# The two parts of the row maxima are transposed by a DMA from SBUF to SBUF

## The chip, the core and the metric

The kernel runs on one core of a Trainium2 chip. Its engines are TensorE (PE: matmuls, and PEld, their weight loads), VectorE (DVE), ScalarE (ACT), GpSimd (POOL) and SyncE (SP, which issues every DMA of this kernel). Matmuls write to PSUM; all other tiles here lie in SBUF or in device memory. The metric is the device time of one execution in microseconds (us), the median over several runs. A profile of one execution shows what each engine did and what it waited for.

## What is computed

A layer norm of x, sliding-window attention (32 heads of 20 values, window 256, 2048 positions) over it, an MLP with squared ReLU as a gate, and a residual. Cut to that:

```python
xn = _layernorm(x)                                # x: 1 x 2048 x 640
q, k, v = split(xn @ wqkv)                        # 32 heads, Dh = 20
scores = einsum("bhqd,bhkd->bhqk", q, k) * Dh ** -0.5
scores = where(0 <= i - j < 256, scores, -1e9)
s = merge(einsum("bhqk,bhkd->bhqd", softmax(scores), v)) @ wo
h = relu(xn @ w1 + b1)                            # 640 -> 1536
g = silu((h * h) @ w2 + b2)
return x + s * g
```

## The kernel before

The first part of the program (about 120 us) normalizes x, transposes it, makes the values and the first queries and keys, and stores all of them to device memory. Numbers are kept as two or three parts of lower precision (a high part and rests), so that products come out nearly exact.

The second part is the attention loop. Heads go in 16 pairs p, and each pair in 16 blocks q of 128 queries. One step s of the loop starts one block: p, q = divmod(s, 16). In step s:

- `scores` (matmul on line 432) makes the scores of the block for both heads of the pair, queries on partitions, each in a PSUM buffer of the tag "s"; there are two such buffers.
- `maxima` (line 444) takes each row's maximum on VectorE. After every fourth block (a **group** of four blocks, both heads: 8 maxima in each of 128 rows) lines 448 and 449 write the negated maxima in two bf16 parts to `mp`, one of two tiles of 128 x 128 of which 16 columns are in use.
- In the next step, s = 4, 8, 12 and so on, `max_rows` turns `mp`, so that the 16 columns become 16 rows. Line 458 is a TensorE transposition with an identity matrix. It stands between the two score matmuls of that step, and writes to a corner of the first one's PSUM buffer. Line 462 (VectorE, behind that step's maxima) copies 16 rows to `mrow`, and two DMAs carry them into two additional rows of the queries `qs`. These DMAs go through `post`, and so leave SP in the middle of the step (line 542).
- `scores_t` (line 476) works on the block that began 9 steps ago (LAG): it computes the scores again, keys on partitions, with the two additional rows subtracting the maximum. It reads three query blocks, so the rows of a group are first wanted in the third step after the one that turned them; for the first group of a pair in the fifth.
- `exps`, `high`, `low` and `values` (lines 483 to 511) make the exponentials, their two parts, and the products with the values, over the steps that follow. `normed` divides and stores the outputs o.

The program's order on each engine is written out by hand: it is the order of these calls. TensorE's remaining time is filled by a generator, `fill`: the queries and keys of later pairs (qkps), then the MLP's first and second matmuls (hps, yps) and, after the loop, the output projection (wops). A fixed amount of such work is taken out twice in each step, whatever the time. The filler's evacuations run on ScalarE, VectorE and GpSimd, and its loads, stores and weight pieces go through SP as well: `post_all` issues what has been posted, and `issue` starts weight loads and bulk loads, each at the top and in the middle of a step. SP issues in order, so a DMA that waits holds up all those behind it.

Of the kernel before, what the change touches and what calls it, by code (L numbers as in the profile page):

```python
# [7 lines left out]
F32 = mybir.dt.float32  # L8
F32R = mybir.dt.float32r
BF16 = mybir.dt.bfloat16  # L10
# [4 lines left out]
P = 128  # L15
# [5 lines left out]
NT = S // P  # L21
# [6 lines left out]
KR = NPART * DH  # L28
# [23 lines left out]
def attn_mlp_kernel(ctx: ExitStack, tc, x, wqkv, wo, w1, b1, w2, b2, out):  # L52
    nc = tc.nc
    PSUM = bass.MemoryType.PSUM
    const = ctx.enter_context(tc.tile_pool(name="const", bufs=1))
    bigp = ctx.enter_context(tc.tile_pool(name="bigp", bufs=8))
    pmm = ctx.enter_context(tc.tile_pool(name="pmm", bufs=3, space=PSUM))
    pat = ctx.enter_context(tc.tile_pool(name="pat", bufs=2, space=PSUM))
# [21 lines left out]
    ident = const.tile([P, P], F32, name="ident")  # L80
    nc.gpsimd.memset(ident, 1.0)
    nc.gpsimd.affine_select(ident, ident, pattern=[[1, P]], compare_op=ALU.is_equal, fill=0.0, base=0, channel_multiplier=-1)
    identb = const.tile([P, P], BF16, name="identb")
    nc.gpsimd.tensor_copy(identb, ident)
    mask = const.tile([P, 3 * P], F32, name="mask")
    nc.gpsimd.memset(mask, 0.0)

# [22 lines left out]
    qs = [at.tile([P, 2, S], BF16, name="qs0")]  # L110
# [4 lines left out]
    def ones_rows(i):  # L115
        nc.sync.dma_start(ks[i][KR:KR + 2].rearrange("a h (c n) -> a (h c) n", n=2 * P), ones.unsqueeze(1).to_broadcast([2, S // P, 2 * P]))

    def pair_loads(p, half):
        r = []
        cols = slice(half * HS, (half + 1) * HS)  # L120
        for h in range(2):
            src = slice((2 * p + h) * DH, (2 * p + h + 1) * DH)
            for w, st in (("k", ks), ("q", qs)):
                r.append((st[p % 2][0:KR, h, cols], qk_d[w][src, :, cols].rearrange("d a n -> (d a) n")))
        return r

    with tc.tile_pool(name="ph1v", bufs=2) as p1v, tc.tile_pool(name="ph1", bufs=2) as p1, tc.tile_pool(name="ph1x", bufs=4) as p1b, tc.tile_pool(name="ph1w", bufs=1) as p1w:
# [136 lines left out]
        with tc.manual_schedule(engines={E_.PE, E_.Activation, E_.DVE, E_.Pool, E_.SP}):  # L264
# [90 lines left out]
            for w in "kq":  # L355
                ps = pmm.tile([P, BT // 2], F32, tag="mm", name="qkps")
# [15 lines left out]
            for b in range(NB):  # L372
# [16 lines left out]
                for w in "kq":  # L389
                    ps = pmm.tile([P, BT], F32, tag="mm", name="qkps")  # L390
# [21 lines left out]
    at2 = ctx.enter_context(tc.tile_pool(name="at2", bufs=2))  # L412
# [5 lines left out]
    def load_v(p):  # L418
        vp = at2.tile([P, NB, 4, 2, VW], BF16, tag="vp", name=f"vp_{p}")
        nc.sync.dma_start(vp.rearrange("p b t h w -> p (b t h w)"), v_d[:, p].rearrange("p b n -> p (b n)"))  # L420
        vps[p] = vp

    mts = {}

    def scores(p, q, between):
        i = p % 2
        k0 = max(0, q - 2)
        nk = (q - k0 + 1) * P
        r = []
        for hh in range(2):  # L430
            ps = pat.tile([P, 4 * P], F32, tag="s", name="sps")
            nc.tensor.matmul(ps[:, :nk], qs[i][0:KR, hh, q * P:(q + 1) * P], ks[i][0:KR, hh, k0 * P:k0 * P + nk], start=True, stop=True)  # L432
            r.append(ps)
            if not hh:
                rows = between and between(ps)
        return (r, nk), rows

    def maxima(p, q, r, nk):
        if q % 4 == 0:
            mts[p, q // 4] = at2.tile([P, 2, 4], F32, tag="mt", name="mt")  # L440
        mt = mts[p, q // 4]
        for hh in range(2):
            junk = at2.tile([P, 3 * P], BF16, tag="junk", name="junk")
            nc.vector.tensor_tensor_reduce(out=junk[:, :nk], in0=r[hh][:, :nk], in1=mask[:, 3 * P - nk:], scale=1.0, scalar=-3.0e38, op0=ALU.add, op1=ALU.max, accum_out=mt[:, hh, q % 4:q % 4 + 1])  # L444
        if q % 4 == 3:

            mp = mps[q // 4 % 2][:, 0:16].rearrange("p (h a b) -> p h a b", h=2, a=2)
            nc.vector.tensor_scalar(mp[:, :, 0, :], mt, -1.0, None, ALU.mult)
            nc.vector.scalar_tensor_tensor(mp[:, :, 1, :], mt, -1.0, mp[:, :, 0, :], ALU.mult, ALU.subtract)
            mts[p, q // 4] = mps[q // 4 % 2]  # L450

    def max_rows(p, g, tp=None):
        i = p % 2
        mp = mts.pop((p, g))
        if tp is None:
            tp = pat.tile([P, 4 * P], F32, tag="s", name="mtp")
        tp = tp[:, 3 * P:3 * P + P // 2].bitcast(BF16)
        nc.tensor.transpose(tp, mp, identb)

        def rest():  # L460
            mrow = at2.tile([16, P], BF16, tag="mrow", name="mrow")
            nc.vector.tensor_copy(mrow, tp[0:16, :])
            for hh in range(2):
                post(qs[i][KR:KR + 2, hh, g * 512:(g + 1) * 512].rearrange("o (a n) -> o a n", a=4), mrow[8 * hh:8 * hh + 8, :])
        return rest

    pts = {}
    ots = {}

# [67 lines left out]
    def post(dst, src):  # L537
        posts.append((dst, src))

    def post_all():  # L540
        for dst, src in posts:
            nc.sync.dma_start(dst, src)
        posts.clear()
# [4 lines left out]
    def mark():  # L548
        return flushed[0] + len(pending)

    def flush(upto=None):
        for f in late[:]:
            f()
        late.clear()
        while pending and (upto is None or flushed[0] < upto):
            flushed[0] += 1
            pending.pop(0)()
# [23 lines left out]
    def issue(amount):  # L581
        credit[0] = min(credit[0] + amount, amount)
        while credit[0] > 0 and start_pieces(1):
            credit[0] -= 1.0
        while bulk and credit[0] > 0:
            cost, fn = bulk.pop(0)
            fn()
            credit[0] -= cost

    def bulk_dma(cost, dst, src):  # L590
        item = (cost, lambda: nc.sync.dma_start(dst, src))
        bulk.append(item)
        return item

    def ensure_bulk(items):
        for it in items:
            if it in bulk:
                bulk.remove(it)
                it[1]()
# [25 lines left out]
    def tick():  # L625
        for f in release(1):
            f()
            held[0] -= 1
# [304 lines left out]
    def fill(amount):  # L933
        state[1] += amount
        while state[0] < state[1]:
            c = next(fl, None)
            if c is None:
                state[1] = state[0]
                return
            state[0] += c  # L940

    per = total / (steps - 1)
    with tc.manual_schedule(engines={E_.PE, E_.Activation, E_.DVE, E_.Pool, E_.SP}):
        load_v(0)
        exs, phs, norm, loads = {}, {}, [], []

        def at_step(n):
            return divmod(n, NT) if 0 <= n < NP * NT else None

        for s in range(steps):  # L950
            state[2] = s
            post_all()
            issue(RATE)
            a, b, c, d, e = (at_step(s - lag) for lag in (0, LAG, LAG + 1, LAG + 2, LAG + 3))
            if a:
                p, q = a
                if q == 0:
                    ensure_bulk(loads)
                if s == 2:
                    ones_rows(1)  # L960
                if q == 2 and p < NP - 1:
                    loads = [bulk_dma(0.7, *l) for l in pair_loads(p + 1, 0)]
                if q == LAG and p < NP - 1:
                    loads += [bulk_dma(0.7, *l) for l in pair_loads(p + 1, 1)]
                if q == LAG + 4 and p < NP - 1:
                    load_v(p + 1)
            rows = between = None
            if s % 4 == 0 and 0 < s <= NP * NT:
                def between(tp=None, s=s):
                    return max_rows((s - 1) // NT, (s - 1) % NT // 4, tp)  # L970
            if a:
                sc, rows = scores(p, q, between)
            elif between:
                rows = between()
            if a:
                maxima(*a, *sc)
            if rows:
                rows()
            if norm:
                norm.pop()()  # L980
            fill(EARLY_FILL * per)
            if b:
                stp = scores_t(*b)
            post_all()
            issue(RATE)
            flush()
            if d:
                low(*d)
            tick()
            if b:  # L990
                exs[b] = (exps(*b, *stp), stp[1])
            if c:
                high(*c, *exs.pop(c))
            while norm:
                norm.pop()()
            fill((1 - EARLY_FILL) * per + SWING * (-1) ** (s - LAG - 3))
            if e and e[1] % 2:
                values(e[0], e[1] - 1)
                values(*e)
                if e[1] % 4 == 3:  # L1000
                    norm.append(normed(e[0], e[1] // 4))
        while norm:
            norm.pop()()
        state[2] = 10 ** 6
        for _ in fl:
            post_all()
            flush(mark() - 1)
        flush()
        post_all()
# [23 lines left out]
```

## Time and profile before

| | |
|---|---|
| Median of 3 runs | 936.42 us (935.34 to 936.46) |
| Span of the profiled execution, first to last instruction | 933.0 us |
| Transpositions on line 458 | 64 |
| Copies to mrow on line 462 | 64 |
| Row DMAs on line 542 | 128, of 2.0 KB each |
| Loop, by the first and last scores of line 432 | 120.0 to 818.3 us |

How to read the lines quoted below. An instruction is named by engine, line and operation, then the tile written <- the tiles read. In a timeline the first number is the start in us from the span's start and the second the duration; x is how many were merged, and brackets hold the idle time before it and what ended it. In a group's line the numbers behind the bar are busy us, mean ns of one, and idle us before it. SPq is SP's queue: the duration is that of the issue, not of the transfer. Line numbers without further words are those of the kernel before.

### The profile page before, as it was taken

The page shows a single profiled execution, that of the slowest core. Times are in us where ns is not written, and L with a number is a line of the kernel's source. Part 1 is how long each engine was busy: PE and PEld are TensorE (multiplying, and loading weights), DVE is VectorE, ACT ScalarE, POOL GpSimd, SP SyncE. Part 2 cuts the span into 40 slices and gives each one's busy share as a digit, 9 for nine tenths or more (in the row PEclk, how much of TensorE's full clock was granted, in tenths as well). Part 3 has the DMA queues.
Part 4 walks back from the last instruction along what each step waited for, and adds up shares of the span by engine and source line. Part 5 has one row for each costly group of instructions (what it writes and reads, how often), then busy time and mean ns, then how long its engine had stood idle before and what let it go on. Part 6 is the DMA issues. An engine that isn't in the chain of part 4 may idle for free.

```text
span 933.0 us, 23236 instructions
## 1 busy us (share of the span) xinstructions
PE 907.9 (97%) x8352; PEld 792.4 (85%) x8352; DVE 758.8 (81%) x2031; ACT 670.1 (72%) x1282; POOL 538.1 (58%) x832
## 2 busy tenths in 40 slices
PE   8999999999998999999999999899999999999998
PEld 7899976666666798898899897798998898889998
DVE  7694478989999988888888889988888888866554
ACT  5354339888988887887887788887787888795221
POOL 6010017887878876866766775766775766782000
PEclk9999999999999999999999999999999999999999
DMA  6998686777789553343445266445354544128873
GB/s 230 307 398 301 207 265 195 225 223 234 231 252 307 180 164 94 116 141 99 142 122 150 74 193 204 150 150 161 113 163 141 159 131 143 56 74 280 292 276 124
DMA packets 150072, 174.11 MB, mean 187 GB/s; under 512 B 44420, under 2 KB 112068, under 8 KB 148932
## 3 DMA queue, kind: packets, MB, share of 16 engines
q1 hardware_dynamic: 149956, 172.63, 57.8%
q8 instruction: 65, 1.06, 0.5%
q14 instruction: 51, 0.42, 0.1%
HBM read 101.39 MB, written 70.91 MB: 185 GB/s over the span
## 4 chain that ended last, share of the span: by engine, by line
PE 71%; DVE 15%; ACT 4%; issue 4%; DMA 3%; POOL 2%; SPq 0%; POOLq 0%; DVEq 0%; ACTq 0%
PE yps L816 15%; PE hps L562 14%; PE wops L562 8%; PE sps L432 7%; PE vps L243 6%; PE stps L476 6%; PE ops L511 6%; PE qkps L562 5%; DVE junk L444 4%; DVE pl L497 3%; DVE w L659 2%; PE qkps L201 1%; ACT p L483 1%; ACT ph L491 1%; DVE st L142 1%
## 5 line engine op out<-in xcount | busy, mean ns | idle before, releaser
L483 ACT ACTIVATE p<-stps,ebias 128x384 f32<-128x384 f32 (+2 forms) x512 | 258.0, 556 | 89.7 <-PE stps L476 84.6
L444 DVE CUSTOM_DVE_ANT_0 junk<-sps,mask 128x384 bf16<-128x384 f32 (+2 forms) x512 | 251.0, 527 | 62.3 <-PE sps L432 55.9
L497 DVE TENSOR_TENSOR pl<-p,ph 128x768 f16<-128x768 f32 (+2 forms) x256 | 249.2, 973 | 1.8 <-ACT ph L491 1.7
L562 PE MATMUL hps<-xb,w 128*128 128x256 f32 x1440 | 230.8, 300 | 0.0
L816 PE MATMUL yps<-w,hh 128*128 128x320 f32 x1152 | 227.3, 331 | 0.0
L484 POOL TENSOR_SCALAR_AFFINE_SELECT p<-p 128x256 f32<-128x256 f32 x256 | 149.2, 583 | 120.9 <-ACT p L483 111.3
L491 ACT ACTIVATE ph<-p 128x768 f16<-128x768 f32 (+2 forms) x256 | 205.8, 804 | 13.4 <-POOL p L486 12.0
L562 PEld LDWEIGHTS hps<-xb,w 128*128 128x128 f32 x1440 | 194.6, 190 | 11.9 <-issue 2.1
L816 PEld LDWEIGHTS yps<-w,hh 128*128 128x128 f32 x1152 | 179.7, 189 | 11.8 <-issue 2.4
L432 PE MATMUL sps<-ks,qs 120*128 120x384 bf16 (+2 forms) x512 | 128.9, 319 | 8.1 <-DVE mt L444 7.8
L785 POOL TENSOR_TENSOR hh<-sq,hh 128x256 fp32r<-128x256 f32 x96 | 103.4, 1081 | 51.5 <-DVE sq L784 25.5
L476 PE MATMUL stps<-qs,ks 122*128 122x384 bf16 (+2 forms) x512 | 123.9, 322 | 1.0 <-ACT p L483 0.4
L486 POOL TENSOR_SCALAR_AFFINE_SELECT p<-p 128x256 f32<-128x256 f32 x224 | 111.9, 500 | 0.0
L511 PE MATMUL ops<-vp,ph 128*128 128x61 bf16 x1440 | 101.1, 193 | 0.0
L511 PE MATMUL ops<-vp,pl 128*128 128x61 bf16 x1440 | 99.8, 192 | 0.0
L511 PEld LDWEIGHTS <-ph 128*128 128x128 f16 x1440 | 86.0, 97 | 14.5 <-issue 7.4
L511 PEld LDWEIGHTS <-pl 128*128 128x128 f16 x1440 | 87.8, 98 | 0.0
L243 PE MATMUL vps<-wv,xT 128*128 128x320 f32 x480 | 72.1, 309 | 0.6 <-POOL wv L179 0.3
L243 PEld LDWEIGHTS vps<-wv,xT 128*128 128x128 f32 x480 | 70.5, 188 | 1.3 <-POOL wv L179 0.6
L562 PE MATMUL wops<-wo,oT 128*128 128x320 f32 x384 | 62.5, 311 | 0.3 <-DVE oT L104 0.3
L739 POOL TENSOR_TENSOR slo<-srt,shm 128x512 bf16<-128x512 f32 x32 | 39.5, 1236 | 37.7 <-PE sps L432 24.2
L432 PEld LDWEIGHTS <-qs 120*128 120x128 bf16 x512 | 36.3, 98 | 27.9 <-issue 13.7
(112 smaller groups left out, 1334.5 us busy)
## 6 DMA issues: line engine op xcount, KB each, us to landing
xb<-xs SPq DMA_DIRECT2D x32, 640.0 KB
ks<-k_d SPq DMA_DIRECT2D x64, 240.0 KB
qs<-q_d SPq DMA_DIRECT2D x64, 240.0 KB
xs<-xT SPq DMA_DIRECT2D x8, 1280.0 KB
y<-ysb SPq DMA_DIRECT2D x32, 320.0 KB
q_d<-shm SPq DMA_DIRECT2D x38, 256.0 KB
v_d<-vt SPq DMA_DIRECT2D x8, 976.0 KB
vp<-v_d SPq DMA_DIRECT2D x16, 488.0 KB
```

Source lines behind the costliest of these rows:

```text
L243: nc.tensor.matmul(ps, xT[xp][b][:, c * BT + t * P: c * BT + (t + 1) * P], wv[wp][:, c, nh * HALF:(nh + 1) * HALF], start=n == 1, stop=n = ...
L432: nc.tensor.matmul(ps[:, :nk], qs[i][0:KR, hh, q * P:(q + 1) * P], ks[i][0:KR, hh, k0 * P:k0 * P + nk], start=True, stop=True)
L444: nc.vector.tensor_tensor_reduce(out=junk[:, :nk], in0=r[hh][:, :nk], in1=mask[:, 3 * P - nk:], scale=1.0, scalar=-3.0e38, op0=ALU.add, op ...
L476: nc.tensor.matmul(ps[:, :n], ks[i][0:KR + 2, hh, kb * P:(kb + 1) * P], qs[i][0:KR + 2, hh, kb * P:kb * P + n], start=True, stop=True)
L483: nc.scalar.activation(p32[:, hh, :n], r[hh][:, :n], AF.Exp, scale=SCALE, bias=ebias)
L484: nc.gpsimd.affine_select(p32[:, :, 0:P], p32[:, :, 0:P], pattern=[[0, 2], [1, P]], compare_op=ALU.is_ge, fill=0.0, base=0, channel_multip ...
L486: nc.gpsimd.affine_select(p32[:, :, 2 * P:], p32[:, :, 2 * P:], pattern=[[0, 2], [-1, P]], compare_op=ALU.is_gt, fill=0.0, base=0, channel ...
L491: nc.scalar.activation(ph[:, :, :n], p32[:, :, :n], AF.Copy)
L497: nc.vector.tensor_sub(pl[:, :, :n], p32[:, :, :n], ph[:, :, :n])
L511: nc.tensor.matmul(ot[:, q % 4, hh, :], t[:, hh, (q - k) * P:(q - k + 1) * P], vp[:, k // 4, k % 4, hh, :], start=m == 1, stop=m == 2 * le ...
L562: nc.tensor.matmul(ps, a, b_, start=j == 0, stop=j == n - 1)
L816: nc.tensor.matmul(pss[nh], hs[fc][:, hp, tt * P:(tt + 1) * P], lin1(wt2, (wp * NFH + fc) * D + nh * HALF, HALF), start=fc == 0 and j == 0 ...
```

## The change

`max_rows` no longer uses TensorE or VectorE. At the same place in the program (the top of steps 4, 8, 12 and so on) SP issues a transposing DMA of all of `mp`, 128 x 128 bf16, into `mrow`, which is now 128 x 128 as well. The two row DMAs are issued by a new function, `place_rows`, at the top of the following step, behind that step's posted and bulk DMAs; SP waits there until the transposing DMA has landed. The two score matmuls of a step stand side by side again, `scores` and `maxima` are called without the parts in between, and the identity matrix in bf16 (one copy on GpSimd at the start) is gone. Line numbers behind it become smaller by 2 to 14.

```diff
-    identb = const.tile([P, P], BF16, name="identb")
-    nc.gpsimd.tensor_copy(identb, ident)
...
-    def scores(p, q, between):
+    def scores(p, q):
...
             r.append(ps)
-            if not hh:
-                rows = between and between(ps)
-        return (r, nk), rows
+        return r, nk
...
-    def max_rows(p, g, tp=None):
-        i = p % 2
-        mp = mts.pop((p, g))
-        if tp is None:
-            tp = pat.tile([P, 4 * P], F32, tag="s", name="mtp")
-        tp = tp[:, 3 * P:3 * P + P // 2].bitcast(BF16)
-        nc.tensor.transpose(tp, mp, identb)
-
-        def rest():
-            mrow = at2.tile([16, P], BF16, tag="mrow", name="mrow")
-            nc.vector.tensor_copy(mrow, tp[0:16, :])
+    def max_rows(p, g):
+        mrow = at2.tile([P, P], BF16, tag="mrow", name="mrow")
+        nc.sync.dma_start_transpose(mrow, mts.pop((p, g)))
+        mrows.append((p, g, mrow))
+
+    def place_rows():
+        while mrows:
+            p, g, mrow = mrows.pop(0)
             for hh in range(2):
-                post(qs[i][KR:KR + 2, hh, g * 512:(g + 1) * 512].rearrange("o (a n) -> o a n", a=4), mrow[8 * hh:8 * hh + 8, :])
-        return rest
-
+                nc.sync.dma_start(qs[p % 2][KR:KR + 2, hh, g * 512:(g + 1) * 512].rearrange("o (a n) -> o a n", a=4), mrow[8 * hh:8 * hh + 8, :])
+
+    mrows = []
...
-            rows = between = None
+            place_rows()
             if s % 4 == 0 and 0 < s <= NP * NT:
-                def between(tp=None, s=s):
-                    return max_rows((s - 1) // NT, (s - 1) % NT // 4, tp)
+                max_rows((s - 1) // NT, (s - 1) % NT // 4)
             if a:
-                sc, rows = scores(p, q, between)
-            elif between:
-                rows = between()
-            if a:
-                maxima(*a, *sc)
-            if rows:
-                rows()
+                maxima(*a, *scores(*a))
```

## The prediction

> **What bounds the kernel now.** I read the page first: the busy shares, then the chain of work that ended last.
>
> ```profile
> PE 907.9 (97%) x8352; PEld 792.4 (85%) x8352; DVE 758.8 (81%) x2031; ACT 670.1 (72%) x1282; POOL 538.1 (58%) x832
> PE 71%; DVE 15%; ACT 4%; issue 4%; DMA 3%; POOL 2%; SPq 0%; POOLq 0%; DVEq 0%; ACTq 0%
> ```
>
> TensorE carries 71% of the chain and VectorE 15%, so an operation taken from either can count, but only where that engine is the one waited for. So I cut the span into stretches; the columns are the stretch, its length, each engine's busy time with its instructions, the clock, the DMA share and GB/s.
>
> ```profile
> core 0: us, PE busy (x) PEld busy (x) DVE busy (x) ACT busy (x) POOL busy (x), PEclk, DMA share, GB/s
> 144.00:222.00 78.00, 77.25 (x646) 53.51 (x644) 71.49 (x188) 68.91 (x126) 65.19 (x89) 1.00 0.73 229
> 276.00:327.00 51.00, 45.17 (x429) 35.33 (x426) 49.43 (x120) 44.39 (x85) 42.16 (x54) 1.00 0.76 244
> 327.00:554.00 227.00, 225.97 (x2393) 204.04 (x2388) 194.00 (x572) 182.34 (x353) 157.84 (x261) 1.00 0.44 132
> 554.00:605.00 51.00, 45.95 (x457) 39.02 (x454) 48.90 (x122) 43.31 (x82) 36.32 (x52) 1.00 0.53 162
> 605.00:823.00 218.00, 217.17 (x2290) 195.99 (x2288) 186.81 (x548) 175.22 (x338) 147.98 (x249) 1.00 0.45 136
> ```
>
> Two long stretches, 327 to 554 and 605 to 823, are TensorE's: it is busy 443.1 of 445 us. Two short ones, 276 to 327 and 554 to 605, are VectorE's: it is busy 98.3 of 102 us, TensorE 91.1. In the first third (144 to 222) TensorE leads, with the DMA engines busy 0.73 of the time. The transpositions, all on line 458, lie so:
>
> ```profile
> 276.00:327.00 51.00, 0.92 (x4) 0.40 (x5) 1.00 0.76 244
> 327.00:554.00 227.00, 4.71 (x22) 2.17 (x22) 1.00 0.44 132
> 554.00:605.00 51.00, 0.93 (x5) 0.39 (x4) 1.00 0.53 162
> 605.00:823.00 218.00, 4.52 (x21) 1.98 (x20) 1.00 0.45 136
> ```
>
> 43 of the 64 groups of four query blocks are in TensorE's stretches, 9 in VectorE's.
>
> **The issue slot on TensorE.** A group in a TensorE stretch:
>
> ```profile
> 745.59 0.33 PE L432 MATMUL sps<-ks,qs 120*128 120x384 bf16 x1
> 745.76 0.22 PE L458 MATMUL sps<-identb,mp 128*128 128x128 bf16 x1
> 745.82 0.33 PE L432 MATMUL sps<-ks,qs 120*128 120x384 bf16 x1
> ```
>
> The transposition's row lasts 0.22 us, but matmuls overlap: it starts 0.17 behind its predecessor, and the next score matmul starts 0.06 behind it. It costs 0.06 us of TensorE, and 64 x 0.06 = 3.8 us leave the bounding engine.
>
> The Trainium skill speaks against this part: VectorE: DVE Perf Modes, "The three transpose paths", gives 390 ns for a 128x128 bf16 transposition on TensorE and 1309 ns for one by DMA, and its rules prefer TensorE where PSUM will do. By its 390 ns the term would be 25 us, an estimate; the row's 0.06 decides, since the pipeline hides the rest.
>
> **The wait of the transposition.** It needs both parts of the maxima, and the second score matmul stands behind it. The groups of these lines, with busy time, mean ns, and idle time before; behind them the waits of its weight loads (us, times, longest), in the whole span and in VectorE's two stretches:
>
> ```profile
> L458 PE MATMUL sps<-identb,mp 128*128 128x128 bf16 x63 | 14.0, 222 | 6.5 <-DVE mp L449 6.4
> L449 DVE SCALAR_TENSOR_TENSOR mp<-mt,mp 128x8 bf16<-128x8 f32 x64 | 12.2, 190 | 2.2
> L448 DVE TENSOR_SCALAR mp<-mt 128x8 bf16<-128x8 f32 x64 | 14.0, 219 | 2.2
> ...
> PEld L458 <- DVE mp L449: 10.8, 15, 1.3
> ...
> PEld L458 <- DVE mp L449: 3.3, 4, 1.1
> ...
> PEld L458 <- DVE mp L449: 1.9, 3, 1.0
> ```
>
> A sample of it, from a VectorE stretch:
>
> ```profile
> 300.76 0.08 DVE L444 DVE_READ_ACCUMULATOR2_ANT mt<- 128x1 f32 x1
> 301.09 0.33 PE L432 MATMUL sps<-ks,qs 120*128 120x384 bf16 x1
> 301.86 0.17 DVE L449 SCALAR_TENSOR_TENSOR mp<-mt,mp 128x8 bf16<-128x8 f32 x1
> 302.09 0.23 PE L458 MATMUL sps<-identb,mp 128*128 128x128 bf16 x1 [0.67 <-DVE mp L449]
> 302.15 0.33 PE L432 MATMUL sps<-ks,qs 120*128 120x384 bf16 x1
> ```
>
> The order of TensorE there, before (sps are the scores, mp the two parts; the filler's matmuls follow):
>
> ```order
> L511 MATMUL ops<-vp_3509,pl 128x61
> L432 LDWEIGHTS qs_120
> L432 MATMUL sps<-ks_121,qs_120 128x384
> L458 LDWEIGHTS mp_102
> L458 MATMUL sps<-identb,mp_102 128x128
> L432 LDWEIGHTS qs_120
> L432 MATMUL sps<-ks_121,qs_120 128x384
> L562 MATMUL hps<-xb_0_4183,w_0_1_4199 128x256
> ```
>
> and with the change:
>
> ```order
> L504 MATMUL ops<-vp_3494,pl 128x61
> L430 LDWEIGHTS qs_118
> L430 MATMUL sps<-ks_119,qs_118 128x384
> L430 LDWEIGHTS qs_118
> L430 MATMUL sps<-ks_119,qs_118 128x384
> L555 MATMUL hps<-xb_0_4167,w_0_1_4183 128x256
> ```
>
> The two score matmuls now stand together. The second still waits for its PSUM buffer, hence for the second maximum of the step before (done at 300.84 here), but no longer for the two small operations behind that: 0.22 + 0.19 = 0.41 us by their means, 1.18 in the sample. The wait itself is 6.5 us by the matmul's row, 10.8 by its weights'. What is late next is VectorE: the next step's scores wait for this step's maxima, which depend on VectorE's own pace. So for the 7 waits in VectorE's stretches I count nothing. The other 8 can give 8 x 0.41 = 3.3 us; I take half, 1.6 us, because TensorE, once ahead, meets its next wait sooner. The ends are 0 and 6.5.
>
> **The copy on VectorE.**
>
> ```profile
> L462 DVE COPY mrow<-sps 16x128 bf16<-16x128 bf16 x63 | 13.0, 207 | 0.0
> L432 PEld LDWEIGHTS <-qs 120*128 120x128 bf16 x512 | 36.3, 98 | 27.9 <-issue 13.7 <-DVE mrow L462 4.4 <-DMA q_d<-shm 0.3
> ```
>
> The 64 copies take 13.2 us, but outside VectorE's stretches they stand beside TensorE's work. Inside, they are on the path (weight loads of line 432 wait 4.4 us for them): 9 x 0.21 = 1.9 us. Taking all of the 4.4 is the upper end, 0 the lower.
>
> **What is added on SP's queue.** Each group adds one DMA, and the two small row DMAs move from the middle of a step to the top of the next, behind a wait for that DMA. Here is SP's queue for the group at 156.80, before (q_d, k_d are stores of queries and keys, o of outputs, raw a weight load):
>
> ```order
> L542 DMA k_d<-slo 128x512
> L542 DMA qs_120<-mrow 2x4x128 x2
> L542 DMA q_d<-shm 128x2x512
> L542 DMA q_d<-slo 128x512
> L542 DMA q_d<-shm 128x2x512
> L542 DMA q_d<-shm 128x512
> L542 DMA o_85<-on 128x4x40
> L644 DMA raw<-in_A_wqkv_dram 128x5x128 x2
> ```
>
> and with the change:
>
> ```order
> L535 DMA k_d<-slo 128x512
> L450 DMA_TRANSPOSE mrow<-mp_101 128x128
> L535 DMA q_d<-shm 128x2x512
> L535 DMA q_d<-slo 128x512
> L535 DMA q_d<-shm 128x2x512
> L535 DMA q_d<-shm 128x512
> L535 DMA o_85<-on 128x4x40
> L637 DMA raw<-in_A_wqkv_dram 128x5x128
> L457 DMA qs_118<-mrow 2x4x128 x2
> ```
>
> The rows now go behind four stores, an output store and a load. The wait added at the rows holds up what is queued behind it, here the second load and the key stores. The trace gives the times of those neighbours, and of the first consumer of the rows, the transposed scores three steps later:
>
> ```profile
> 158.42 1.27 SPq L542 DMA_DIRECT2D qs<-mrow  x2
> 162.96 0.39 SPq L542 DMA_DIRECT2D o<-on  x1
> 163.39 1.15 SPq L644 DMA_DIRECT2D raw<-in_A_wqkv_dram  x2
> 165.40 0.50 PE L476 MATMUL stps<-qs,ks 122*128 122x384 bf16 x2
> ```
>
> The rows' issue would move from 158.42 to about 163.96 (the first of the two loads ends half of 1.15 behind 163.39). The 1.27 us that the rows no longer take ahead of the stores I set against the transposition's issue and the stores' own waits for their data, and change nothing for it. How long they take to land, in a quiet stretch:
>
> ```profile
> 747.21 1.29 SPq L542 DMA_DIRECT2D qs<-mrow  x2
> 747.20:748.20 1.00, 1.00 (x9) 1.00 (x8) 1.00 (x3) 1.00 (x3) 0.58 (x2) 1.00 0.00 0
> 748.20:749.20 1.00, 1.00 (x9) 0.84 (x7) 0.77 (x2) 0.53 (x1) 1.00 (x3) 1.00 0.02 4
> 749.20:749.40 0.20, 0.20 (x3) 0.11 (x2) 0.20 (x3) 0.00 (x0) 0.20 (x1) 1.00 0.00 0
> 749.60 0.39 SPq L542 DMA_DIRECT2D o<-on  x1
> 754.76 0.39 PE L476 MATMUL stps<-qs,ks 122*128 122x256 bf16 x2
> ```
>
> They move their 4 KB within 2.0 us of the issue. So at 156.80 they land at 165.96, 0.6 us after TensorE wants them. I charge that once, 0.6 us. In the quiet group the rows would follow the output store, 749.60 + 0.39 = 749.99, and land at 752.0, 2.8 us ahead of need.
>
> The transposing DMA itself is not in the trace. Nearest are the rows' 2.0 us for two DMAs of 2 KB and, for ten times its 32 KB, the first load of x:
>
> ```profile
> 0.80 1.35 SPq L134 DMA_DIRECT2D xt<-in_A_x_dram  x3
> 3.79 0.89 DVE L142 BATCH_NORM_STATS2 st<-xt 128x6 f32<-128x320 f32 x2 [3.79 <-DMA xt<-in_A_x_dram]
> ```
>
> 2.99 us from issue to use. I take 2 to 3 us. (The Trainium skill's 1309 ns, from the section named above, would lie below that.) Nothing shows that a turned 32 KB goes at a copy's pace, so the far end stays open; but in the quiet group it may be issued at 745.59, when the parts were ready, and the rows would not go before 749.99 anyway: 4.4 us cost nothing, and 4.4 + 2.8 = 7.2 cost TensorE nothing. I cost it at nothing; if the cover is gone, each us beyond 7.2 is paid by 48 groups (the first group of a head pair is wanted two steps later).
>
> **The sum.** 3.8 + 1.6 + 1.9 - 0.6 = 6.7 us off the profiled span of 933.0, so 926.3. The median of the runs, 936.4, stands 3.4 above that span. I keep the distance: 929.7 us.
>
> **The rivals.**
> - More of it comes off. All of the waits (6.5) and of the copies' 4.4 are kept: 3.8 + 6.5 + 4.4 = 14.7, so 921.7. For it: TensorE is 97% busy. Against: half of those waits are in VectorE's stretches.
> - Nothing to be measured. Waits return at the next scores, the copies' time stays idle, and late rows eat the slots: 3.8 - 3 = 0.8, so 935.6.
> - Slower: the rows come late. Place: the transposed scores in the stretch with stores, 144 to 222 (7 groups, 5 of them not first of a pair). The rows are issued at 7.2 us of the 8.6 that they have, so it decides from a landing over 1.4. At 2.99 us each is 1.6 late; if every row waits as long again behind the stores (5.98), 4.6 late: 5 x 4.6 = 23 us against 7.3 gained, so 952. Against: other groups have no load ahead of the rows. A sentence of the Trainium skill bears on it: DMA: Bandwidth & Descriptors, "Queues, rings and completion order", has each DMA engine take its descriptors in ring order, so a late issue also queues behind those stores; no row here shows a row DMA queued.
> - Slower: the transposition isn't the quick transfer that it is meant to be. At 10 us 48 x 2.8 = 134 us are added, about 1060. Nothing in the trace speaks for it.
>
> **How the numbers follow.** Forecast, 924 to 934.5: 0.56; more off, 918 to 924: 0.11; nothing: 0.15; rows late: 0.14, of which half below 941; slow transposition: 0.04. I leave out the last, the worse half of the late rows and the far part of the gain: 921 to 941. A measurement here tells about 0.2%, 1.9 us, from no change: faster 0.67, same 0.15, slower 0.18.
>
> **What would show it.** Right: the second score matmul starts 0.17 behind the first in a group's step; VectorE loses 13 us of busy time; TensorE's two stretches are each about 1.3 us shorter (22 x 0.06); no wait of the transposed scores for a DMA. Wrong: waits of the transposed scores for the rows, in the first third above all; SP waiting over 4 us for the transposition; more waits of converted weights or stores behind SP.

## Result and the profile after

| | before | after |
|---|---|---|
| Median of 4 runs each, on one chip | 936.44 us (935.34 to 936.64) | 957.34 us (955.66 to 958.6) |
| Span of the profiled execution | 933.0 us | 956.7 us |

The ratio is 1.0227, 95% interval 1.0211 to 1.0242: the change costs 2.3%. From the page of the changed kernel, its busy times and its chain of waits:

```profile
PE 913.2 (95%) x8288; PEld 794.2 (83%) x8288; DVE 756.8 (79%) x1967; ACT 672.2 (70%) x1282; POOL 524.7 (55%) x831
PE 73%; DVE 10%; DMA 8%; ACT 3%; issue 3%; POOL 2%; SPq 1%; DVEq 0%; POOLq 0%; ACTq 0%
```

TensorE has 64 matmuls fewer, yet it is busy 5.3 us longer (913.2 against 907.9; the last section shows why). Its share of the longer span fell from 97 to 95%, and DMA in the chain rose from 3 to 8%. The waits of the changed kernel name the transfer (us, times, longest; line 469 is `scores_t`):

```profile
PEld L469 <- DMA qs<-mrow: 26.3, 21, 4.3
PE stps L469 <- DMA qs<-mrow: 18.8, 15, 3.8
...
ACT w L649 <- DMA raw<-in_B_w_dram: 5.5, 2, 3.6
```

Before, TensorE had no wait for a DMA of rows. (The two rows tell of the same groups: a weight load and its matmul both stand, so they are not added.) SyncE's queue of the changed kernel waits at the rows for the transposition:

```profile
SPq L457 <- DMA mrow<-mp: 16.7, 10, 3.7
```

Where in the program it went is read from the last 344 of the 512 score matmuls, steps 84 and later (the first and last start stand behind the durations), before and then after:

```profile
L432 PE MATMUL sps<-ks,qs x344: 216/327/340, 348.3 to 818.3; 120*128 120x384 bf16 x152, 120*128 120x128 bf16 x10, 120*128 120x256 bf16 x10
```

```profile
L430 PE MATMUL sps<-ks,qs x512: 216/326/543, 122.7 to 842.0; 120*128 120x384 bf16 x149, 120*128 120x128 bf16 x11, 120*128 120x256 bf16 x11
L430 PE MATMUL sps<-ks,qs x344: 216/326/339, 368.8 to 842.0; 120*128 120x384 bf16 x152, 120*128 120x128 bf16 x10, 120*128 120x256 bf16 x10
```

The loop's first 84 steps took 348.3 - 120.0 = 228.3 us before and 368.8 - 122.7 = 246.1 after, 17.8 more. The other 172 steps took 470.0 and 473.2, 3.2 more. The remaining 2.7 us lie ahead of the loop, and by the other runs they are not the change's. Near 43 us TensorE waits 2.7 us for VectorE (1.2 before), and from 44 to 48 us its granted clock is 0.57 (1.00 before). e7 below, whose program is the old one up to the loop, has the same (a wait of 2.0 us, a clock of 0.57 from 43 to 47 us, the loop from 121.8), while e2 and e10, which have the new one, start the loop at 120.8 and 120.7. 17.8 + 3.2 + 2.7 = 23.7, the difference of the spans.

How a group is late, in the chain of the changed kernel at one of its longest waits (start, us, what):

```profile
294.87 0.61 DVE pl L490
295.49 5.67 DMA mrow<-mp
301.22 4.03 DMA qs<-mrow
305.30 0.82 PE stps L469 x2
```

The transposition takes 5.67 us from its issue until the rows can go (SyncE issues four other DMAs in between and waits for the last 1.3 us), the rows another 4.03, and only then the transposed scores run. The two transfers stand in series.

### The profile page after: what moved, and what is told of

It reads as the page before. It is cut to its first block, busy times and chain, and to the rows that moved or that the text cites. A ratio compares the mean times of both kernels' runs of the same rounds, so it can differ in the third digit from the quotient of the medians.

```text
span 956.7 us, 23127 instructions
## 1 busy us (share of the span) xinstructions
PE 913.2 (95%) x8288; PEld 794.2 (83%) x8288; DVE 756.8 (79%) x1967; ACT 672.2 (70%) x1282; POOL 524.7 (55%) x831
## 2 busy tenths in 40 slices
DMA packets 160312, 176.22 MB, mean 184 GB/s; under 512 B 54660, under 2 KB 122308, under 8 KB 159172
## 4 chain that ended last, share of the span: by engine, by line
PE 73%; DVE 10%; DMA 8%; ACT 3%; issue 3%; POOL 2%; SPq 1%; DVEq 0%; POOLq 0%; ACTq 0%
PE yps L809 15%; PE hps L555 14%; PE wops L555 7%; PE qkps L555 7%; PE ops L504 7%; PE stps L469 7%; PE sps L430 7%; PE vps L241 6%; DMA mrow<-mp 3%; DMA qs<-mrow 3%; DVE junk L440 3%; PE qkps L199 2%; DVE pl L490 2%; DVE w L652 1%; DMA xt<-in_A_x_dram 1%
## 5 line engine op out<-in xcount | busy, mean ns | idle before, releaser
L490 DVE TENSOR_TENSOR pl<-p,ph 128x768 f16<-128x768 f32 (+2 forms) x256 | 253.1, 989 | 1.8 <-ACT ph L484 1.7
L477 POOL TENSOR_SCALAR_AFFINE_SELECT p<-p 128x256 f32<-128x256 f32 x256 | 145.1, 567 | 146.8 <-ACT p L476 139.4
L484 ACT ACTIVATE ph<-p 128x768 f16<-128x768 f32 (+2 forms) x256 | 205.6, 803 | 12.2 <-POOL p L479 10.7
L469 PE MATMUL stps<-qs,ks 122*128 122x384 bf16 (+2 forms) x512 | 126.1, 325 | 23.4 <-DMA qs<-mrow 18.8
L430 PE MATMUL sps<-ks,qs 120*128 120x384 bf16 (+2 forms) x512 | 125.4, 319 | 10.1 <-DVE mt L440 9.9
L778 POOL TENSOR_TENSOR hh<-sq,hh 128x256 fp32r<-128x256 f32 x96 | 103.2, 1079 | 54.8 <-DVE sq L777 25.6
L479 POOL TENSOR_SCALAR_AFFINE_SELECT p<-p 128x256 f32<-128x256 f32 x224 | 109.2, 488 | 0.0
L469 PEld LDWEIGHTS <-ks 122*128 122x128 bf16 x512 | 31.0, 99 | 58.4 <-DMA qs<-mrow 26.3
L241 PE MATMUL vps<-wv,xT 128*128 128x320 f32 x480 | 72.1, 309 | 0.6 <-POOL wv L177 0.3
L555 PE MATMUL qkps<-xT,wgkh 128*128 128x512 f32 x160 | 60.5, 437 | 0.0
```

The source lines that it names most:

```text
L241: nc.tensor.matmul(ps, xT[xp][b][:, c * BT + t * P: c * BT + (t + 1) * P], wv[wp][:, c, nh * HALF:(nh + 1) * HALF], start=n == 1, stop=n = ...
L469: nc.tensor.matmul(ps[:, :n], ks[i][0:KR + 2, hh, kb * P:(kb + 1) * P], qs[i][0:KR + 2, hh, kb * P:kb * P + n], start=True, stop=True)
L477: nc.gpsimd.affine_select(p32[:, :, 0:P], p32[:, :, 0:P], pattern=[[0, 2], [1, P]], compare_op=ALU.is_ge, fill=0.0, base=0, channel_multip ...
L479: nc.gpsimd.affine_select(p32[:, :, 2 * P:], p32[:, :, 2 * P:], pattern=[[0, 2], [-1, P]], compare_op=ALU.is_gt, fill=0.0, base=0, channel ...
L484: nc.scalar.activation(ph[:, :, :n], p32[:, :, :n], AF.Copy)
L490: nc.vector.tensor_sub(pl[:, :, :n], p32[:, :, :n], ph[:, :, :n])
```

## Experiments

Each ratio is to the kernel before, run on the same chip as the experiment; its medians there were 935.62 to 936.38 us.

| Run | median, us | ratio to before, 95% |
|---|---|---|
| e1: TensorE transposition, rows where the change puts them | 945.84 | 1.0081 to 1.0119 |
| e8: TensorE transposition, rows ahead of all in the next step | 935.05 | 0.9988 to 1.0006 |
| e3: transposing DMA, rows ahead of all in the next step | 960.65 | 1.0241 to 1.0286 |
| e2: transposing DMA, rows in the same step | 969.07 | 1.0327 to 1.0379 |
| e6: transposing DMA, rows issued by GpSimd | 973.43 | 1.0392 to 1.0463 |
| e5: before, and an unused transposing DMA a group | 939.1 | 1.0022 to 1.0059 |
| e9: e8, and an unused transposing DMA whose landing SyncE awaits | 967.46 | 1.0311 to 1.0353 |
| e11: e9 without that wait, as many issues | 951.77 | 1.0141 to 1.0189 |
| e10: e3, transposing DMA issued by ScalarE | 944.93 | 1.0064 to 1.0107 |
| e7: TensorE for the first 20 groups, e3's way for the other 44 | 932.95 | 0.9953 to 0.9978 |

### The place of the rows alone (e1, then e8)

e1 keeps TensorE's transposition and the copy, and only issues the rows where the change does:

```diff
-                post(qs[i][KR:KR + 2, hh, ...], mrow[8 * hh:8 * hh + 8, :])
+                mrows.append((qs[i][KR:KR + 2, hh, ...], mrow[8 * hh:8 * hh + 8, :]))
...
+            place_rows()
             if s % 4 == 0 and 0 < s <= NP * NT:
```

> Three theories of the 21 us that the change costs. Place: the rows are late because they are issued at the top of the next step, behind output stores and value loads on SP's queue. Landing: the transposing DMA itself takes 3 to 6 us where the DMA engines are loaded (it took 1.4 us in quiet stretches of the changed kernel), and the rows wait for it. Issue: each transposing DMA holds SP for 1.13 us and adds 32 KB of traffic. This run keeps TensorE's transposition and VectorE's copy and only moves the two row DMAs to the top of the next step. Place alone: the transposed scores wait for rows in about a dozen groups, most of them with a value load ahead of the rows, 7 to 15 us in all, 943 to 955 us. Landing or issue: no such waits to speak of (under 3 us), 934 to 939 us. Both place and landing: 939 to 946 us.

945.84 us, 9.8 more than before on that chip (936.07): the place alone costs nearly half of what the change costs (20.9). Its last 344 scores:

```profile
L432 PE MATMUL sps<-ks,qs x344: 217/326/339, 351.8 to 827.2; 120*128 120x384 bf16 x152, 120*128 120x128 bf16 x10, 120*128 120x256 bf16 x10
```

With the first at 120.8, the first 84 steps took 231.0 us, 2.7 more than before, and the last 172 took 475.4, 5.4 more. So the place costs mainly behind the first third, and most of the changed kernel's 17.8 us in the first third are something else. SyncE's queue and the transposed scores of e1, at one of the late groups:

```profile
377.42 0.39 SPq L548 DMA_DIRECT2D o<-on  x1
377.86 0.56 SPq L597 DMA_DIRECT2D xb<-xs  x1
378.51 0.57 SPq L420 DMA_DIRECT2D vp<-v_d  x1
379.14 1.38 SPq L469 DMA_DIRECT2D qs<-mrow  x2
```

```profile
383.88 0.52 PE L482 MATMUL stps<-qs,ks 122*128 122x384 bf16 x2 [1.46 <-DMA qs<-mrow]
```

An output store, a load of 640 KB (xb) and one of 488 KB (vp) were issued just ahead, and the rows, whose 4 KB took 2.0 us in the quiet stretch, are waited for until 4.74 us after their issue. e8 puts the same rows ahead of them, at the very top of the step:

```diff
             state[2] = s
+            place_rows()
             post_all()
```

> TensorE transposition and copy as before; only the two row DMAs stand at the very top of the next step on SyncE's queue, ahead of that step's stores and loads. Theory 'the 10 us of the place are the store or value load that stands ahead of the rows on the same queue': without one ahead the rows land in about 2 us, the waits of the transposed scores fall from 20 us (12.3 + 7.8 in the run with the place alone) to under 5, and the time is 936 to 939 us. Theory 'half a step later is late by itself': waits stay at 15 us or more, 943 to 947 us. If the first holds, what the kernel with the transposing DMA at this same place lost (24 us) is the transposing DMA's landing alone.

935.05 us, within 0.1% of before, and no row on the rows' DMA in its waits. The first theory holds: half a step later is early enough; it is the transfers ahead of the rows on the queue that make them late.

### The transposing DMA with the rows moved forward (e2, e3)

If the place were all, the changed kernel would be mended by the same move. e3 issues the rows at the top of the next step, e2 in the same step:

```diff
             state[2] = s
+            place_rows()
             post_all()
...
-            place_rows()
             if s % 4 == 0 and 0 < s <= NP * NT:
```

> The DMA transposition, rows at the top of the next step but ahead of everything that this step issues (output store, weight and bulk loads, value load). Place: the waits behind value loads go (390, 563, 700, 744, 790 us in the changed kernel; 5 us or more), those behind the middle of the step stay: 935 to 945 us. Landing: only the value-load groups change, 945 to 953 us. Issue: 952 to 958 us.

> The DMA transposition, but the rows are issued in the middle of the same step, ahead of that step's stores and of the next step's output store and value load. Place: the waits for rows fall from 18.8 us to under 3, and the time to 929 to 935 us. Landing: SP stands still until the transposition has landed, the waits in the groups with heavy DMA traffic (139, 243, 277, 290 us in the changed kernel) remain, 6 us or more, and loads queued behind are late too: 940 to 950 us. Issue: some 5 us less than the changed kernel at most, 950 to 957 us.

Both became slower than the change itself, 960.65 and 969.07 us, beyond every range that was expected of them; the theory that the place is all falls. e8 and e3 have the rows at the same place and differ in how `mp` is turned: 25.6 us for the transposing DMA. SyncE's queue of e3 at a late group:

```profile
278.60 1.31 SPq L457 DMA_DIRECT2D qs<-mrow  x2
280.01 0.40 SPq L535 DMA_DIRECT2D o<-on  x1
280.51 0.45 SPq L535 DMA_DIRECT2D q_d<-shm  x1
281.05 0.43 SPq L535 DMA_DIRECT2D q_d<-slo  x1
281.53 0.98 SPq L535 DMA_DIRECT2D q_d<-shm  x2
282.55 1.42 SPq L637 DMA_DIRECT2D raw<-in_B_w_dram  x3
284.07 1.52 SPq L535 DMA_DIRECT2D k_d<-shm  x2
285.69 0.88 SPq L535 DMA_DIRECT2D k_d<-slo  x1
286.66 1.70 SPq L450 DMA_TRANSPOSE mrow<-mp  x1
291.59 1.31 SPq L457 DMA_DIRECT2D qs<-mrow  x2
```

and of e3 the second part of the maxima on VectorE, and the matmul that wants the rows:

```profile
280.15 0.32 DVE L445 SCALAR_TENSOR_TENSOR mp<-mt,mp 128x8 bf16<-128x8 f32 x1
```

```profile
293.32 0.50 PE L469 MATMUL stps<-qs,ks 122*128 122x384 bf16 x1 [4.07 <-DMA qs<-mrow]
```

The parts are ready at 280.47. SyncE, still behind from the rows of the group before, works through its stores and loads without a gap and comes to the transposition at 286.66, 6.2 us late. It stands until 291.59, 4.9 us from the issue. TensorE has by then waited for the rows since 289.25 (293.32 - 4.07).

Is it the turn on the queue or the landing? Group by group in e3's timelines, SyncE issues the transposition a median of 5.2 us behind its data in the first 20 groups (at most 10.5), and 0.03 us behind it in the other 44 (at most 2.9). From that issue until SyncE goes on with the rows pass 2.3 to 6.6 us in the first 20 (median 4.2), and 2.2 to 7.1 in the others (median 3.3). So the landing is little longer in the first third than behind it; what differs is that SyncE comes late. SyncE's waits at the rows in e3, in the whole span:

```profile
SPq L457 <- DMA mrow<-mp: 153.5, 64, 5.8
```

Every one of the 64 groups waits, against 10 in the changed kernel: where the rows stood later, most of the landing was covered by the DMAs in between. But behind the first third the waits do not matter:

```profile
L430 PE MATMUL sps<-ks,qs x344: 216/326/339, 377.9 to 844.5; 120*128 120x384 bf16 x152, 120*128 120x128 bf16 x10, 120*128 120x256 bf16 x10
```

844.5 - 377.9 = 466.6 us for the last 172 steps, 3.4 less than before. All of e3's loss lies ahead of them. e8, with the rows at the same place and TensorE's transposition, takes 470.0 us for these steps (348.6 to 818.6), as before, so the 3.4 us come from the transposition.

### The wait moved to GpSimd (e6)

```diff
-                nc.sync.dma_start(qs[p % 2][KR:KR + 2, hh, ...], mrow[8 * hh:8 * hh + 8, :])
+                nc.gpsimd.dma_start(qs[p % 2][KR:KR + 2, hh, ...], mrow[8 * hh:8 * hh + 8, :])
```

> The changed kernel, with the two row DMAs of each group issued by GpSimd instead of SyncE at the same place of the program; SyncE keeps the transposition and never waits for its landing. Theory 'SyncE stands still' (what costs is that SyncE waits for the landing, 16.7 us in all in the changed kernel, and that the rows stand behind an output store or a value load on its queue): the waits of the rows move to GpSimd, which has 45% of its time free, SyncE's waits for the transposition are 0, the waits of the transposed scores for rows fall from 45 us (26.3 + 18.8) to under 15, and the time comes to 936 to 945 us. Theory 'landing' (what costs is that the transposition itself lands 3 to 6 us late under load, whoever issues the rows): the waits of the transposed scores in the first third stay over 20 us, the time stays at 950 to 957. Theory 'GpSimd becomes the bound': its masking waits behind the rows for the landing, ScalarE's second parts and the value products wait for it, and the time is above 957.

973.43 us, the worst. The third theory came true, though not by waiting alone: GpSimd spends 72.1 us on issuing rows, and stands 39.4 before them:

```profile
L457 POOL DMA_DIRECT2D qs<-mrow x128 | 72.1, 564 | 39.4 <-DMA mrow<-mp 18.9 <-issue 10.4 <-PE qkps L555 5.7
```

In e6's waits ScalarE stands for GpSimd's masks 38.5 us (10.7 in the changed kernel), and TensorE's weight loads for the rows 36.2 us (26.3 there):

```profile
ACT ph L484 <- POOL p L479: 38.5, 35, 6.0
PEld L469 <- DMA qs<-mrow: 36.2, 25, 6.1
```

An engine that works in order passes the wait on to its own work. So this run could not show what freeing SyncE would bring.

### The DMA that nobody waits for, and the wait that nobody needs (e5, e9, e11)

e5 is the kernel before with an unused transposing DMA in each group, where `mp` is turned:

```diff
+        spare = at2.tile([P, P], BF16, tag="spare", name="spare")
+        nc.sync.dma_start_transpose(spare, mp)
```

> The kernel before, with the same 64 transposing DMAs added at the same place and read by nobody: TensorE and VectorE still make the rows, in the middle of the step as before. Issue: SP's 64 x 1.13 = 72 us and the traffic cost 3 us or more, 940 to 948 us. Place or landing: nobody waits for it, 935 to 938 us.

939.1 us over 7 runs, 3 us more than before, between the two ranges: 64 issues and their traffic cost little while nothing waits for them. e9 is e8 (same time as before) with such a spare, and behind the rows at the top of the next step two small unused DMAs that read it:

```diff
+            t = spares.pop(0)
+            back = at2.tile([16, P], BF16, tag="back", bufs=1, name="back")
+            for hh in range(2):
+                nc.sync.dma_start(back[8 * hh:8 * hh + 8, :], t[8 * hh:8 * hh + 8, :])
```

> The kernel of the run with the place ahead of all (TensorE transposition, copy, rows at the top of the next step; same time as before), and to it a spare transposing DMA in each group with two small DMAs that read it, behind the rows at the top of the next step; their output is used by nothing. So SyncE waits for the landing as in the kernel with the transposing DMA at that place (153.5 us of SyncE's waits there), but no row depends on it. Theory 'SyncE standing still': the loads and stores behind the wait come late, and the loss of that kernel (24 us) is here too, 950 to 962 us, waits of converted weights for raw loads among them. Theory 'the rows themselves are late': SyncE waits over 100 us here too and nobody minds; the time is 936 to 942 us, waits of the transposed scores for rows under 5 us.

967.46 us, 31.1 more and above both ranges, though no row depends on the spare. The waits of e9 at SyncE, and at the engines:

```profile
SPq L484 <- DMA spare<-mp: 46.8, 34, 4.0
```

```profile
PEld L495 <- DMA qs<-mrow: 20.7, 17, 5.7
ACT w L675 <- DMA raw<-in_B_w_dram: 19.8, 6, 5.9
PE stps L495 <- DMA qs<-mrow: 14.8, 11, 5.3
```

SyncE waited less than half as long as expected (46.8, not over 100), but the rows, made by TensorE in good time, are late all the same, and so are the raw weights. "The rows themselves are late" falls; a SyncE that is held up suffices. e9 also adds 128 small issues, however. e11 takes the wait out and keeps the issues: the small DMAs read VectorE's rows instead of the spare.

```diff
-            t = spares.pop(0)
+            spares.pop(0)
+            t = last_rows[0]
```

> The run with the wait alone (967.5 us), with one thing changed: the two small unused DMAs of each group read the rows that VectorE copied instead of the spare transposition, so SyncE issues as many DMAs at the same places (64 spare transpositions of 1.13 us and 128 small ones of 0.67 us, 158 us of SyncE's time more than before) and waits for the landing of none. Theory 'SyncE standing still': the 46.8 us of waits for the spare are gone and with them most of the 31 us: 936 to 948 us. Theory 'SyncE is full': its issue time alone puts it behind in the first third, the rows and the raw weights come late as in the run with the wait: 955 to 968 us. In between the two shares are read off the difference to 967.5 us and to 936 us.

951.77 us, between the two theories: the wait costs 967.46 - 951.77 = 15.7 us, the issues with their traffic 951.77 - 936.38 = 15.4. Both shares are clear of the noise. The second is for 192 issues a run; the change adds 64, which e5 puts at 3.

### Another queue for the transposition (e10)

```diff
-        nc.sync.dma_start_transpose(mrow, mts.pop((p, g)))
+        nc.scalar.dma_start_transpose(mrow, mts.pop((p, g)))
```

> The kernel with the transposing DMA and the rows at the top of the next step, with the transposing DMA issued by ScalarE instead of SyncE; the rows stay on SyncE. Theory 'own queue' (the transposition lands late because it stands behind loads and stores on SyncE's queue): on a queue of its own it lands in about 1.4 us as in the quiet stretch, SyncE's waits for it fall from 153.5 us to under 40, late rows vanish, 936 to 945 us, less what ScalarE loses by issuing (64 times about 1.1 us, beside the 30% it has free). Theory 'engines' (the DMA engines are full in that stretch, whichever queue): SyncE's waits stay over 100 us and the time at 955 to 970 us. Theory 'late issue' (SyncE came late to issue it): waits fall only in the first third, by the 4 to 7 us that SyncE runs behind there, 940 to 952 us.

944.93 us, 15.7 less than e3. A group of e10 in the same stretch: the second part, ScalarE's issue, and SyncE's rows:

```profile
271.25 0.32 DVE L445 SCALAR_TENSOR_TENSOR mp<-mt,mp 128x8 bf16<-128x8 f32 x1
```

```profile
272.01 1.13 ACTq L450 DMA_TRANSPOSE mrow<-mp  x1
```

```profile
274.05 0.91 SPq L535 DMA_DIRECT2D k_d<-slo  x1
278.15 1.28 SPq L457 DMA_DIRECT2D qs<-mrow  x2
```

The transposition is issued 0.4 us behind its data (6.2 in e3), but not landed sooner: 6.1 us later. "Own queue" had the time right, at the edge of its 936 to 945, and the reason wrong: a queue of its own does not make the transfer quick (from its issue until SyncE goes on with the rows pass a median of 4.9 us in e10's first 20 groups, 4.2 in e3's). "Late issue" fits the 0.4 us and the time too, but both had SyncE's waits fall, and they rose:

```profile
SPq L457 <- DMA mrow<-mp: 318.5, 61, 8.8
```

So the total of SyncE's waits does not measure the loss. Of the transposed scores' waits 1.9 us of weight loads and 0.8 of matmuls are left for rows. What still makes e10 8.6 us slower than before lies in its first 84 steps: they take 240.9 us (120.7 to 361.6), 12.6 more than before, and the last 172 take 468.2, 1.8 less. There TensorE waits for ScalarE's exponentials:

```profile
PE stps L469 <- ACT p L476: 10.8, 13, 2.2
```

10.1 of these 10.8 us lie ahead of 346 us; before, the row stands at 0.4 us in the whole span. Three such waits are followed by a spell at half clock (last section). Which of ScalarE's tasks makes it late (its 64 issues of 1.12 us, 5.9 us of waits for raw weights, or something else) was not taken apart.

### TensorE in the first third, the DMA behind it (e7)

```diff
-            if s % 4 == 0 and 0 < s <= NP * NT:
+            if s % 4 == 0 and FIRST <= s <= NP * NT:    # FIRST = 84
+                max_rows_dma((s - 1) // NT, (s - 1) % NT // 4)
+            elif s % 4 == 0 and 0 < s <= NP * NT:
                 def between(tp=None, s=s):
```

with e3's placement of the rows for the groups turned by DMA.

> The kernel before for the first 20 groups (TensorE transposition, copy by VectorE, rows in the same step), and from the 21st group on (44 groups) the transposing DMA with the rows at the top of the next step. Theory 'the loss lies in the first third, where SyncE and the DMA engines are loaded; behind it the change saves a slot of 0.06 us of TensorE a group': 44 times 0.06 to 0.07, 2.6 to 3.1 us off, no wait of the transposed scores for rows over 1 us behind step 84: 932.5 to 934.5 us, ratio 0.9965 to 0.998. Theory 'the loss is spread over all groups, and hidden by the early one': late rows behind step 84 too, 940 us or more. Theory 'the slot costs nothing when it is full': 936, same as before.

932.95 us (before 935.62): 2.7 us less, ratio 0.9966. It beats the kernel before by a third of a per cent, and the changed one by more. Its last 344 scores, and those of the stretch that is VectorE's (554 to 605) with the steps to 616, the latter for before as well:

```profile
L432 PE MATMUL sps<-ks,qs x344: 216/326/339, 350.0 to 816.6; 120*128 120x384 bf16 x152, 120*128 120x128 bf16 x10, 120*128 120x256 bf16 x10
...
L432 PE MATMUL sps<-ks,qs x42: 217/323/338, 553.8 to 615.9; 120*128 120x384 bf16 x34, 120*128 120x128 bf16 x4, 120*128 120x256 bf16 x4
```

```profile
L432 PE MATMUL sps<-ks,qs x42: 219/323/339, 553.9 to 615.7; 120*128 120x384 bf16 x34, 120*128 120x128 bf16 x4, 120*128 120x256 bf16 x4
```

It has 466.6 us for the last 172 steps, as e3 has, 3.4 less than before. In VectorE's stretch nothing came off (62.1 against 61.8).

## Why the prediction was wrong

The forecast was 929.7 us, the range 921 to 941; 957.34 was measured. By its steps:

- **The issue slot on TensorE: right, and right in size.** The second score matmul stands 0.17 us behind the first in the changed kernel (two of 0.33 us in 0.50):

```profile
746.79 0.50 PE L430 MATMUL sps<-ks,qs 120*128 120x384 bf16 x2
```

  44 groups of 0.06 make 2.6 of the 3.4 us that e3 and e7 gain behind step 84. By the 390 ns of the Trainium skill's VectorE: DVE Perf Modes ("The three transpose paths") it would have been 44 x 0.39 = 17 us, an estimate; the trace decides against it.
- **The wait of the transposition**, 1.6 in all: at most the other 0.8 us of the 3.4. The kernels whose first third is undisturbed use TensorE there, so the rest of this term was not seen.
- **The copy on VectorE**, 1.9: nothing came off in the one VectorE stretch that could be seen. VectorE's busy time fell by 2.0 us, not by the 13 that I named as a sign. The 64 copies are gone, but the subtractions that make `pl` took 3.9 us more (253.1 against 249.2); the rest was not followed up.
- **"I cost it at nothing": the step that failed.** I covered the transposing DMA with 7.2 us of a quiet group and took that cover for all. Where it was read it held: behind step 84 the transposition is issued at once (median 0.03 us in e3), SyncE goes on at most 7.1 us later, and e7 loses nothing there. In the first third there is no such cover: the transposition comes late to its turn on SyncE's queue (median 5.2 us in e3, 6.2 in the group shown), SyncE goes on a median of 4.2 us later, not 2 to 3, and the rows follow in series. The price was 25.6 us at e3's place, part of it the half clock that follows the waits, and 15.7 of it is gone when ScalarE issues the transposition. I had written that each us beyond the cover is paid, and never worked the cover out for the loaded stretch. (The 1309 ns for a transposition by DMA in the same section of the Trainium skill lie below every one of these 64 times; the least is 2.2 us.)
- **"I charge that once, 0.6 us": failed too.** I looked at the one group with a weight load ahead of the rows, and wrote of the rival that "other groups have no load ahead of the rows". e1 has the rows late in ten matmul waits, 7.8 us in all, and costs 9.8. Six of the ten, 6.4 us, lie behind step 84, and in five of these a value load (vp) stands ahead of the rows.

The rival of late rows came nearest: 952 by its working, with the first third as its place. It had the direction, about the size, and one half of the mechanism (what stands ahead of the rows), though e1 finds that half mainly behind the first third, so the size is in part luck. It did not have the other, that SyncE itself falls behind by what it issues and waits for, which makes rows and weights late that depend on nothing new (e9). I gave it 0.14. "SP waiting over 4 us for the transposition", named as a sign, did not show in the changed kernel (longest 3.7), since the DMAs in between covered the landing; the sign that did show was the waits of the transposed scores.

From 935.05 (e8) to 960.65 (e3) only the way of turning differs. For the changed kernel the shares are read by stage: of its 17.8 us in the first 84 steps the place makes 2.7 by e1, so some 15 are the transposing DMA's; of its 3.2 us behind them the place makes 5.4 by e1, less the 3.4 that the transposition gains. The sums do not close exactly (5.4 - 3.4 is 2.0, not 3.2), since the place also covers part of the landing (957.34, less than e3).

## What to carry to other kernels

A transfer that replaces an engine's operation is priced where the queue is fullest, not where the cover is largest: count its turn on the queue, its landing and what stands ahead of the next link in the chain, in the stretch where the issuing engine is furthest behind. A queue that works in order makes late everything behind a wait, also what depends on nothing new, so a wait put on it needs a check of all its passengers. Where a change wins a little in one stretch and loses much in another, make it by stretch: e7 took the 3 us and left what e3 lost.

## What the runs showed of the hardware

Short waits of TensorE cost twice. These windows of the changed kernel lie around the ends of two waits of the transposed scores, and the last one is the undisturbed stretch behind the second (stretch, length, busy times, clock, DMA share, GB/s):

```profile
150.00:157.00 7.00, 5.74 (x15) 3.60 (x16) 2.26 (x5) 3.96 (x7) 2.35 (x5) 0.51 0.70 224
303.80:310.50 6.70, 5.20 (x37) 3.71 (x37) 4.58 (x15) 4.17 (x8) 2.59 (x6) 0.50 0.96 329
311.00:318.00 7.00, 7.00 (x62) 5.30 (x61) 4.87 (x11) 6.36 (x12) 5.30 (x10) 1.00 0.64 196
```

The second wait, of 3.58 us in the timeline, ended at 305.30, so it began at 301.72; 2.1 us later the granted clock is 0.50 (half clock), for some 7 us. The slowest score matmul takes 543 ns, 340 before the change. In the two spells TensorE was busy 5.74 and 5.20 us, so by an estimate from the clock some 2.9 and 2.6 us of work were lost on top of the waits. That is 5.5 of the 17.8 us of the first 84 steps. In e3 there are five such spells in these steps, worth some 12 us by the same estimate, which is near half of its 25.6; e1, e5 and e8 have none in the loop.

The Trainium skill (TensorE: Matmul & The Clock Gate, Part 1) gives half clock after an idle window of about 3.4 us. Both waits are that long (3.58, and 3.8 by the longest of the waits' row), though the clock falls before the 3.4 are over. In e10 shorter ones do: three waits of 1.8 to 2.2 us are each followed by some 3.4 us at 0.50, one of them here with its spell:

```profile
296.75 0.95 PE L469 MATMUL stps<-qs,ks 122*128 122x384 bf16 x2 [1.83 <-ACT p L476]
```

```profile
297.50:300.50 3.00, 3.00 (x31) 2.38 (x31) 2.59 (x9) 2.78 (x6) 1.61 (x4) 0.50 0.97 270
```

e1's longest wait for rows, 2.13 us, left the clock at 1.00. So in this case 3.4 us is not the limit, and the runs do not show what decides. No run took the clock apart from the waits.

A transposing DMA of 128 x 128 bf16 from SBUF to SBUF holds its issuing queue for 1.13 us (median of 64, 1.11 to 2.96), against 0.64 for a row DMA, and adds 160 packets: 160312 in the changed kernel, 150072 with TensorE's transposition (e1).
